# A decode step on one core: the first K chunk is loaded in two parts, with the first query weights between them

## The chip, the cores and the metric

The kernel runs on one NeuronCore of a Trainium2 chip. The metric is the device time of one execution in microseconds (us). The engines are TensorE (PE; its weight loads are listed as PEld), VectorE (DVE), ScalarE (ACT), GpSimd (POOL) and SyncE (SP). SyncE issues nearly all loads; the core's sixteen DMA engines carry them out.

## The reference

One token passes a transformer block: attention over a cache of 65,536 positions (32 query heads in 8 groups of 4, one K and one V head for each group), then a gated feed-forward layer. Everything is float32.

```python
# x (1, 1, 512); k_cache, v_cache (1, 8, 65536, 128); wq (512, 4096); wo (4096, 512)
q = (layernorm(x) @ wq)                      # 32 heads of 128
scores = einsum("bhqd,bhkd->bhqk", q, repeat(k, 4)) * 128 ** -0.5
o = einsum("bhqk,bhkd->bhqd", softmax(scores), repeat(v, 4))
h = x + o.reshape(1, 1, 4096) @ wo
n = layernorm(h)
out = h + ((n @ w_gate) * (n @ w_up)) @ w_down   # 512 -> 1792 -> 512
```

K and V hold 268 MB each, so every execution reads some 565 MB.

## The kernel before

The cache is cut by head and by chunk. A chunk is 16,384 positions of one K or V head, laid out by the host as 128 rows of 64 KB, one row for each SBUF partition, 8 MiB in all. A head has four K chunks and then four V chunks. Two buffers, `kv[0]` and `kv[1]`, take the chunks in turn. In K chunks the partition is the head dimension, so every score matmul needs all 128 rows of its columns.

The program is written by hand, one stream of instructions for each engine, with semaphores between them. Python unrolls the streams of SyncE, VectorE and ScalarE over the 8 heads; TensorE runs `head()` in a hardware loop.

SyncE's stream (lines 111 to 147) is a list of loads in one queue. It starts with `wq_sb`, the query weights of head 0 (128 rows of 8 KB, 1 MiB, line 111, semaphore `s_wq`). Then come the chunks, line 131, each behind a wait until TensorE is done with the chunk two places before, since that one had the same buffer. The first two chunks need no such wait. Two chunks before the end of a head, the weights for the output of this head and the query of the next follow (line 121; line 123 for the last head). The last V chunk of all and the feed-forward weights come in pieces, so that the last matmuls can begin early.

TensorE first helps with the layer norm of x (lines 320 to 326), waits for constants from VectorE and for the query weights (`take(s_wq, 16)`, which waits for the count and takes it off again), and enters the loop. In `head()` it computes the query of a head with 16 small matmuls (line 333), waits for VectorE to copy it into `q_pad`, waits for chunk 0 on `s_kv[0]`, and runs 32 matmuls of 512 columns on it (line 343); the same for chunks 1 to 3. After the softmax come the four V chunks (line 371), then the output projection into `attn`.

A DMA adds 16 to its semaphore when all of it has landed. The semaphores `s_kv[0]` and `s_kv[1]` belong to the buffers; `s_wq` is used once in the program.

## Time and profile before

| | before |
|---|---|
| median of 3 runs | 1309.71 us (1309.70 to 1309.72) |
| profiled execution | 1309.92 us |
| its span, first to last instruction | 1308.5 us |
| mean granted TensorE clock | 0.738 |
| DMA in all | 564.80 MB, 432 GB/s over the span |
| busy share of TensorE | 54% |

The busy times, durations and waits in the text come from one profiled execution. "Granted clock" is the share of full speed that TensorE was given. In a row of the timeline the columns are start in us, duration in us, engine, line, operation and operands, how many, and in brackets how long the engine stood idle before and what ended that. In a row of DMA issues they are operands, issuing queue, operation, count, size of one where given, and the median time from issue to landing where the profile has one. A queue's row gives packets, megabytes and the share of the sixteen DMA engines' time.

### The profile page before, as it was taken

The numbers are of one execution on the slowest core, as the hardware profiler recorded it, in microseconds if no ns is written. First come the engines' busy times: TensorE is split into PE (matmuls) and PEld (weight loads), VectorE is DVE, ScalarE is ACT, GpSimd is POOL, SyncE is SP. The second block draws the span as 40 slices with busy tenths as digits, with TensorE's granted clock in tenths as the row PEclk, the third lists the DMA queues.
The fourth block names the chain that finished last, engine by engine and source line by source line (L and its number), as shares of the span: only waits on it lengthen the run. The fifth ranks groups of instructions, "written<-read, shape, count | busy, mean of one in ns | idle before, by whom it ended". The sixth has DMA issues, their size and how long they took to land. (4 is left out here: it accounts for less than half of the span.)

```text
span 1308.5 us, 10559 instructions
## 1 busy us (share of the span) xinstructions
PE 712.9 (54%) x4938; PEld 249.0 (19%) x4938; DVE 73.5 (6%) x181; ACT 47.2 (4%) x102; POOL 2.5 (0%) x13
## 2 busy tenths in 40 slices
PE   5366384553755446563564636636365465655556
PEld 3012031210312112120131202212021121311113
DVE  0000000100001000010000100001000010000101
ACT  0000000100001000010000100001000010000100
POOL 0000000000000000000000000000000000000000
PEclk9777666776767867767767867678677677687778
DMA  9999999999999999999999999999999999999998
GB/s 417 427 435 445 421 445 425 441 425 441 425 441 425 441 429 441 441 429 437 429 439 427 441 425 441 427 441 437 435 435 431 439 417 450 425 441 425 441 420 374
DMA packets 12260, 564.80 MB, mean 432 GB/s; under 512 B 1365, under 2 KB 1369, under 8 KB 2010
## 3 DMA queue, kind: packets, MB, share of 16 engines
q1 hardware_dynamic: 12248, 564.67, 99.7%
q8 instruction: 6, 0.10, 0.0%
q14 instruction: 4, 0.03, 0.0%
q10 hardware_dynamic: 2, 0.00, 0.0%
HBM read 564.66 MB, written 0.00 MB: 432 GB/s over the span
## 5 line engine op out<-in xcount | busy, mean ns | idle before, releaser
L343 PE MATMUL psc<-kv,q_pad 128*32 128x512 f32 x2048 | 294.6, 740 | 256.2 <-PEq L315 256.2
L371 PE MATMUL pva<-kv,pt 128*16 128x512 f32 x2048 | 280.1, 707 | 276.9 <-PEq L315 276.8
L343 PEld LDWEIGHTS psc<-kv,q_pad 128*32 128x32 f32 x2048 | 81.3, 133 | 463.0 <-issue 463.0
L371 PEld LDWEIGHTS pva<-kv,pt 128*16 128x16 f32 x2048 | 67.1, 110 | 492.7 <-issue 492.7
L210 ACT COPY sc<-psc 128x512 f32<-128x512 f32 x32 | 18.7, 585 | 1144.3 <-PE psc L343 1144.3
L216 DVE TENSOR_REDUCE mx<-sc 128x1 f32<-128x512 f32 x32 | 21.9, 686 | 538.3 <-ACT sc L210 538.3
L333 PEld LDWEIGHTS sm<-xn,wqo_sb 128*128 128x128 f32 x256 | 49.1, 299 | 10.4 <-issue 10.4
L333 PE MATMUL sm<-xn,wqo_sb 128*128 128x1 f32 x256 | 49.8, 329 | 2.2 <-issue 2.2
L250 DVE COPY orow<-pva 128x512 f32<-128x512 f32 x8 | 5.5, 692 | 566.8 <-PE pva L371 566.8
L358 PE MATMUL ptp<-ident,sc 128*128 128x128 f32 x128 | 29.3, 396 | 10.2 <-PEq L315 9.7
L358 PEld LDWEIGHTS ptp<-ident,sc 128*128 128x128 f32 x128 | 21.4, 202 | 15.5 <-issue 14.7
L235 ACT ACTIVATE sc<-sc,nbias 128x512 f32<-128x512 f32 x32 | 22.7, 711 | 20.2 <-DVE nbias L230 20.2
L240 DVE COPY pt<-ptp 128x512 f32<-128x512 f32 x32 | 22.1, 691 | 21.6 <-PE ptp L358 21.6
L363 PE MATMUL pva<-zeros 128*32 128x512 f32 x64 | 12.9, 890 | 0.0
L384 PE MATMUL attn<-wqo_sb,o_pad 128*32 128x512 f32 x64 | 10.8, 749 | 3.4 <-PEq L315 3.4
L378 PE MATMUL sm<-sel_b,orow 128*128 128x4 f32 x64 | 8.2, 252 | 7.2 <-PEq L315 7.2
L378 PEld LDWEIGHTS sm<-sel_b,orow 128*128 128x128 f32 x64 | 7.7, 191 | 14.4 <-issue 14.4
L349 PE MATMUL sm<-ident,m 128*1 128x128 f32 x8 | 2.2, 269 | 13.6 <-PEq L315 13.6
L406 PE MATMUL psc<-kv,hn_pad 128*32 128x448 f32 x64 | 8.2, 651 | 1.9 <-DMA kv<-in_wu 1.0
L361 PE MATMUL sm<-l,ones 128*128 128x4 f32 x16 | 3.9, 312 | 9.6 <-PEq L315 9.6
L351 PE MATMUL sm<-ones,mexp 1*128 1x1 f32 x16 | 3.4, 279 | 5.7 <-PEq L315 5.7
L235 ACT ACTIVATION_READ_ACCUMULATOR sc<-sc,nbias 128x1 f32 x32 | 6.0, 187 | 0.0
(88 smaller groups left out, 68.6 us busy)
## 6 DMA issues: line engine op xcount, KB each, us to landing
wqo_sb<-in_wqo SPq DMA_DIRECT2D x7, 2048.0 KB, 15.2
kv<-in_v SPq DMA_DIRECT2D x1, 4096.0 KB, 21.7
kv<-in_wg SPq DMA_DIRECT2D x1, 3584.0 KB, 18.8
kv<-in_v SPq DMA_DIRECT2D x1, 2048.0 KB, 26.2
kv<-in_v SPq DMA_DIRECT2D x2, 1024.0 KB, 29.1
kv<-in_wu SPq DMA_DIRECT2D x1, 1792.0 KB, 23.0
kv<-in_wu SPq DMA_DIRECT2D x2, 896.0 KB, 25.5
kv<-in_wd SPq DMA_DIRECT2D x1, 1536.0 KB, 19.7
```

What stands on the lines that cost most here:

```text
L210: copies.append(act.tick(act_e.copy(sc[s], psc[s % 2])))
L216: i = dve_e.tensor_reduce(out=mx[:, s:s + 1], in_=sc[s], axis=AX.X, op=ALU.max)
L235: act_e.activation(sc[s], sc[s], AF.Exp, bias=nbias[:, 0:1], scale=SCALE, accum_out=sums[:, s:s + 1]).then_inc(atok, 1)
L240: dve_e.tensor_copy(pt[s].rearrange("p g b h -> p b g h"), ptp[s % 2].rearrange("p (b g h) -> p b g h", b=4, h=REP)).then_inc(tok, 1)
L333: i = mm(sm[0][:, r:r + 1], wq_sb[:, k, r * P:(r + 1) * P], xn[:, k:k + 1], start=(k == 0), stop=(k == KT - 1))
L343: i = mm(psc[s % 2][32 * j:32 * j + 32, :], q_pad[:, 28 - 4 * rs:60 - 4 * rs], kv[s % 2][:, (4 * rs + j) * 512:(4 * rs + j + 1) * 512], st ...
L358: i = pe_e.transpose(ptp[s % 2][:, b * P:(b + 1) * P], sc[s][:, b * P:(b + 1) * P], ident)
L363: mm(pva[32 * j:32 * j + 32, :], zeros[:, 0:32], zeros, start=True, stop=False)
L371: i = mm(pva[32 * j:32 * j + 16, :], pt[n][:, 8 * j + rs, :, :].rearrange("p b h -> p (b h)"), vt[:, w * 512:(w + 1) * 512], start=False, ...
L378: i = mm(sm[0][:, 0:REP], orow[:, b * P:(b + 1) * P], sel_b[:, 4 * b:4 * b + 4], start=(b == 0), stop=(b == 3))
L384: i = mm(attn[32 * r:32 * r + 32, :], o_pad[:, r, :], wo_sb[:, r, :], start=True, stop=True)
L406: i = mm(acc[32 * j:32 * j + 32, :FJ], hn_pad[:, k, :], w[:, o:o + FJ], start=(k == 0), stop=(k == KT - 1))
```

## The change

Chunk 0 of head 0 is no longer one load. Its rows 0 to 15 are the first load of the program, the query weights the second, and its rows 16 to 127 the third. The 16 rows count on the semaphore of the weights, and TensorE waits for both (32 instead of 16) ahead of its loop. `s_kv[0]` gets its 16 from the load of the 112 rows. The bytes, the destination and everything after chunk 0 are unchanged.

```diff
-    sp.dma_start(wq_sb, wq0).then_inc(s_wq, 16)
     done = []
     for h in range(HKV):
         for i in range(2 * NT):
...
-            if h == LAST and i == 2 * NT - 1:
+            if not done:
+                sp.dma_start(kv[0][0:16], kT[0, 0][0:16]).then_inc(s_wq, 16)
+                sp.dma_start(wq_sb, wq0).then_inc(s_wq, 16)
+                sp.dma_start(kv[0][16:P], kT[0, 0][16:P]).then_inc(s_kv[0], 16)
+            elif h == LAST and i == 2 * NT - 1:
...
     pe_e.wait_ge(dve.sem, c_const)
-    take(s_wq, 16)
+    take(s_wq, 32)
```

## The prediction

> **What bounds the kernel now.** I read the page of the profile first: the engine totals, the forty slices and the DMA queues.

> ```profile
> span 1308.5 us, 10559 instructions
> PE 712.9 (54%) x4938; PEld 249.0 (19%) x4938; DVE 73.5 (6%) x181; ACT 47.2 (4%) x102; POOL 2.5 (0%) x13
> DMA  9999999999999999999999999999999999999998
> DMA packets 12260, 564.80 MB, mean 432 GB/s; under 512 B 1365, under 2 KB 1369, under 8 KB 2010
> q1 hardware_dynamic: 12248, 564.67, 99.7%
> ```

> TensorE is busy for 54% of the span and no other compute engine for over 6%. The DMA row is the one without a hole: the sixteen DMA engines are busy nine tenths or more in 39 slices of 40, and SyncE's queue alone fills 99.7% of their time. 564.67 MB at 432 GB/s is 1307 us, which is the span. So the kernel is as long as its loads, and time lost on the DMA engines has no idle time later in which to be made up.

> The next view is the DMA issues, with the summary of line 131, which issues the whole chunks of K and V.

> ```profile
> kv<-in_kT SPq DMA_DIRECT2D x32, 29.2
> kv<-in_v SPq DMA_DIRECT2D x31, 29.9
> wqo_sb<-in_wq SPq DMA_DIRECT2D x1, 1024.0 KB, 4.8
> x_row<-in_xr ACTq DMA_DIRECT2D x1, 2.0 KB
> out_y<-y SPq DMA_DIRECT2D x1, 2.0 KB
> DMA to landing us min/median/max: 23.7/29.4/44.1
> ```

> A chunk is 128 rows of 64 KB, 8.39 MB, and takes 8.39 / 432 = 19.4 us at the mean rate. The median chunk lands 29.4 us after its issue, so it stands about 10 us in the queue behind the chunk before. That is why a late start is not absorbed: when everything slides by some us, each landing, each release by TensorE and each new issue slide with it, and the engines still have work queued.

> The chain of waits, in order of time, shows the same at the end.

> ```profile
> 1283.06 22.84 DMA kv<-in_wd
> 1305.90 0.04 issue
> 1305.94 0.47 PE pva L437 x8
> 1306.41 0.02 issue
> 1306.44 0.29 DVE y L297
> ```

> The last weights land at 1305.90 and under 1 us of arithmetic follows. A shift of the DMA stream is a shift of the end, one for one.

> **The change part by part.** The start is where the edit is. These are rows of the timeline of its first 60 us, then two stretches of the table of windows (their last columns are the granted clock, the DMA share and GB/s).

> ```profile
> 0.73 0.40 SPq L111 DMA_DIRECT2D wqo_sb<-in_wq  x1
> 1.20 53.85 SPq L131 DMA_DIRECT2D kv<-in_kT  x4
> 8.40 0.15 DVE L200 COPY sel_pad<-sel 128x1 f32<-128x1 f32 x1
> 8.93 6.98 PE L333 MATMUL sm<-xn,wqo_sb 128*128 128x1 f32 x32 [2.24 <-issue]
> 15.94 0.16 DVE L213 COPY q_pad<-sm 128x4 f32<-128x4 f32 x1 [7.08 <-PE sm L333]
> 25.01 9.00 PE L343 MATMUL psc<-kv,q_pad 128*32 128x512 f32 x64 [9.11 <-PEq L315]
> 0.00:5.00 5.00, 2.28 (x10) 2.23 (x10) 0.63 (x5) 1.28 (x1) 2.48 (x13) 1.00 0.72 263
> 200.00:300.00 100.00, 50.50 (x349) 15.21 (x349) 6.11 (x14) 4.69 (x11) 0.00 (x0) 0.72 1.00 435
> ```

> One more issue on SyncE. Three loads are issued where there were two. The first took 0.40 us; one more of that size puts the issues of the remaining 112 rows and of chunk 1 about 0.4 us later. The engines then hold the 1 MiB loads in front, 2 x 2.43 us of work (1.05 MB at 432 GB/s each). Cost nothing; without that cover 0.4 us. Nothing is moved on the queues of ScalarE or GpSimd, and no later issue changes.

> The wait for the query weights. TensorE now waits for the 16 rows and the weights together. Before, the weights landed at 0.73 + 4.8 = 5.5 us, and their matmuls began at 8.93, behind the constants that VectorE finished at 8.55: 3.4 us to spare. If the 16 rows take 2.43 us, the weights land at 8.0 and nothing moves. If they take t us, the weights land near 5.5 + t, the query is ready 7.0 + 0.2 us after that, and behind TensorE's wait stands only the work on chunk 0. That chunk comes by the same queue behind the weights and its other 112 rows alone need 7/8 of 19.4 = 17.0 us; 17.0 exceeds 7.2, so the query is always ready first. Cost nothing, whatever t is.

> The 16-row load itself. Same bytes, but they now go to partitions 0 to 15 alone. Every large load of this trace covers all 128 partitions; the narrow ones, one row of x and the output, are 2 KB and show no rate. So bound it from both sides. If only the sixteen DMA engines matter, they take a 64 KB row each at full rate: 2.43 us, no cost. If 432 GB/s is what 128 partitions can take in, 16 of them take an eighth of it and the load lasts as long as a whole chunk, 19.4 us: 17.0 lost. While it lasts nothing else can go, since the weights and the 112 rows stand behind it in the same queue on the same engines. Between factors 1 and 8 no row lies nearer to one end; I take a factor of 4, about the middle: 9.7 us, 7.3 lost. [...]

> The 112-row load. Shared among sixteen engines it is 7 rows an engine instead of 8, so 17.0 us if all go at full rate. [...] Lower bound nothing; with two engines on one way throughout, a factor of 2, 17.0 us lost on the engine that fares worst, and a load has landed only when its last engine is done. [...] An engine that falls behind here has the same bytes left as before and stays behind to the end.

> At the start-up there might be a gain. In the first 5 us 263 GB/s flowed, 1.32 MB, which at 432 GB/s is 3.04 us: 1.96 us went without flow, 0.73 of them ahead of the first issue. A first load with fewer rows could start flowing earlier, by at most 1.2 us and at least nothing; I take nothing.

> Sum: 0 + 0 + 7.3 + 8.5 + 0 = 15.8 us. The profiled execution took 1309.92 us (span 1308.5 and 1.42 around it), so 1325.7; the median of the runs, 1309.71, is 0.21 lower, so **1325.5 us**.

> **The rivals.** The forecast: both loads are slowed, by 12 to 24.3 us together (7.3 plus 5 to 17.0; or 17.0 and little after it, which gives 1326.7 and is told apart by the landing of the 16 rows). For it: the change leaves 112 partitions idle on a resource that is full for 99.7% of the time.

> Only the first load is slow (7 to 12 us, about 1317.0 by 7.3 alone). This is so if the engines are dealt the 112 rows as evenly as the 128. It decides at the place where the 112-row load ends: all engines done within 17 us of their start.

> Not slower. The DMA engines, not the partitions, are the limit: sixteen rows keep sixteen engines at full rate, both small loads pass in 4.9 us, and the only difference left is the earlier first flow, 0 to 1.2 us: 1308.5 to 1309.7. It decides if the 16 rows land within about 5 us of their issue, as the 1 MiB of weights did in 4.8. For it: an engine's share of 64 KB is the same in both loads. Against it: nothing in the trace, which has no narrow load of size. [...]

> Much slower. If the 112 rows are dealt row by row, so that at each moment sixteen adjacent rows are written, each seventh goes at the factor 4 of the first load: 7 x 9.7 = 67.9 in place of 17.0, 50.9 lost, with 7.3 before it 58 us: 1367.7. Or both upper bounds hold, 17.0 + 17.0: 1343.7. Against the first: in the wide loads sixteen engines together keep 435 GB/s (the second window), so their rows are not dealt in a way that collides.

> **How the numbers follow.** I give the forecast 0.58, only the first load slow 0.22, not slower 0.11, much slower 0.09. The range from 1316 to 1334 holds the first two: it starts a little below 7.3 lost and ends at 7.3 + 17.0 = 24.3 lost. It leaves out 0.20. A measurement of this kernel tells a difference from none at about 0.2%, 2.6 us. Both slow cases and the much slower one are beyond it: slower 0.89. The whole gain to be had at the start is 1.2 us, so the not-slower case is almost all within it: same 0.10, faster 0.01.

> **What would show it.** Right: the 16-row load lands 10 to 13 us after its issue (about 9.7 and the start-up of some 2.4 that the weights' load had: 4.8 less 2.43); the query's matmuls move from 8.93 to some 16 us, without consequence; chunk 0's scores begin near 41 us instead of 25.01; chunks follow at the old pace; the last weights land some 16 us later; q1's share falls because single engines wait. Wrong: the 16 rows land within 5 us; or chunk 0's scores begin at 32 us (first load alone) or beyond 50 us; or the delay at chunk 0 is there but is smaller at the end, which would mean that the stream has slack that I have not seen.

## The result and the profile after

The changed kernel takes 1331.08 us (median of 5 runs, 1330.26 to 1331.56) against 1309.70 for the kernel before on the same chip: 21.4 us more, a ratio of 1.0161 with a 95% interval of 1.0151 to 1.0172. The profiled execution took 1331.56 us with a span of 1330.2. So it is slower, as forecast, by more than the 15.8 us of the sum and inside the range.

From the page of the kernel after, the span, the DMA slices, the GB/s slices, and SyncE's queue; below them the GB/s slices of the kernel before:

```profile
span 1330.2 us, 10560 instructions
DMA  9999999999999999999999999999999999999998
GB/s 221 353 434 434 441 434 426 437 437 436 424 440 436 433 428 437 436 437 436 428 434 439 434 428 439 436 434 428 438 436 437 434 430 434 439 432 430 439 417 361
q1 hardware_dynamic: 12264, 564.67, 99.6%
```

```profile
GB/s 417 427 435 445 421 445 425 441 425 441 425 441 425 441 429 441 441 429 437 429 439 427 441 425 441 427 441 437 435 435 431 439 417 450 425 441 425 441 420 374
```

A slice is 33 us here. The first ran at 221 GB/s and the second at 353, where the kernel before has 417 and 427; from the third on, the rate is the old one. The row of busy shares shows nothing of this: the share is the time that the packets took, however slow they were, so 99.6% stands where 99.7% stood, and from 15 to 45 us the share is 0.95 at 238 GB/s where the kernel before has 0.97 at 418. The GB/s row has to be read beside it.

The start in the timeline of the kernel after (lines are three to four further down than before; L124, L125 and L126 are the three loads), and the summaries of the three loads, in that order:

```profile
0.74 0.41 SPq L124 DMA_DIRECT2D kv<-in_kT  x1
1.21 0.40 SPq L125 DMA_DIRECT2D wqo_sb<-in_wq  x1
1.65 0.43 SPq L126 DMA_DIRECT2D kv<-in_kT  x1
15.79 6.97 PE L336 MATMUL sm<-xn,wqo_sb 128*128 128x1 f32 x32 [9.09 <-PEq L318]
22.80 0.16 DVE L216 COPY q_pad<-sm 128x4 f32<-128x4 f32 x1 [13.93 <-PE sm L336]
47.47 8.98 PE L346 MATMUL psc<-kv,q_pad 128*32 128x512 f32 x64 [24.71 <-PEq L318]
```

```profile
DMA to landing us min/median/max: 11.9/11.9/11.9
DMA to landing us min/median/max: 14.2/14.2/14.2
DMA to landing us min/median/max: 45.7/45.7/45.7
```

The 16 rows land at 0.74 + 11.9 = 12.6 us, the weights at 15.4, the 112 rows at 47.4. The query is ready at 23.0, and TensorE, whose last query matmul ended at 22.76, stands idle for 24.71 us until chunk 0 is there. The scores of chunk 0 begin at 47.47 where they began at 25.01: 22.5 us later. The end of the chain moves nearly as far: the last weights land at 1327.60 instead of 1305.90, 21.7 us later.

```profile
1304.96 22.64 DMA kv<-in_wd
1327.60 0.04 issue
1327.64 0.47 PE pva L440 x8
```

Two stretches of the windows table tell how the 112 rows went (last column: GB/s), first of the kernel after, then of the kernel before:

```profile
15.00:30.00 15.00, 6.97 (x32) 6.90 (x32) 0.16 (x1) 0.00 (x0) 0.00 (x0) 1.00 0.79 210
30.00:45.00 15.00, 0.00 (x0) 0.00 (x0) 0.00 (x0) 0.00 (x0) 0.00 (x0) 1.00 1.10 267
```

```profile
15.00:30.00 15.00, 5.89 (x37) 2.25 (x40) 0.16 (x1) 0.00 (x0) 0.00 (x0) 1.00 0.97 419
30.00:45.00 15.00, 4.01 (x40) 1.05 (x32) 0.69 (x1) 0.58 (x1) 0.00 (x0) 0.81 0.96 416
```

Together the sixteen engines ran at half rate and a little over it. The trace's packets, one for each row, show that all of them did: in the load of 112 rows a row took 2.8 to 4.9 us (median 4.5), where a row of a whole chunk takes 2.42 in the kernel before. It is not one engine that fell behind. In the first load the sixteen rows, moved side by side, took 8.0 to 9.2 us each.

### The profile page after: what moved, and what is told of

Same layout as the page of the kernel before. It is cut to its first block, busy times and chain, and to the rows that moved or that the text cites. A ratio compares the mean times of both kernels' runs of the same rounds, so it can differ in the third digit from the quotient of the medians.

```text
span 1330.2 us, 10560 instructions
## 1 busy us (share of the span) xinstructions
PE 718.0 (54%) x4938; PEld 250.7 (19%) x4938; DVE 73.5 (6%) x181; ACT 47.2 (4%) x102; POOL 2.5 (0%) x13
## 2 busy tenths in 40 slices
DMA  9999999999999999999999999999999999999998
DMA packets 12276, 564.80 MB, mean 425 GB/s; under 512 B 1381, under 2 KB 1385, under 8 KB 2026
## 3 DMA queue, kind: packets, MB, share of 16 engines
q1 hardware_dynamic: 12264, 564.67, 99.6%
## 5 line engine op out<-in xcount | busy, mean ns | idle before, releaser
L213 ACT COPY sc<-psc 128x512 f32<-128x512 f32 x32 | 18.7, 585 | 1166.6 <-PE psc L346 1166.6
L361 PE MATMUL ptp<-ident,sc 128*128 128x128 f32 x128 | 29.1, 394 | 10.2 <-PEq L318 9.7
L243 DVE COPY pt<-ptp 128x512 f32<-128x512 f32 x32 | 22.1, 691 | 21.4 <-PE ptp L361 21.4
## 6 DMA issues: line engine op xcount, KB each, us to landing
kv<-in_v SPq DMA_DIRECT2D x1, 4096.0 KB, 21.4
kv<-in_v SPq DMA_DIRECT2D x2, 1024.0 KB, 28.9
```

Of the source, the lines that this page charges most:

```text
L213: copies.append(act.tick(act_e.copy(sc[s], psc[s % 2])))
L243: dve_e.tensor_copy(pt[s].rearrange("p g b h -> p b g h"), ptp[s % 2].rearrange("p (b g h) -> p b g h", b=4, h=REP)).then_inc(tok, 1)
L361: i = pe_e.transpose(ptp[s % 2][:, b * P:(b + 1) * P], sc[s][:, b * P:(b + 1) * P], ident)
```

## The experiments

The theory was that the partitions a load writes set its rate. Its rivals were the cut as such (a third load, a small one first, a later wait of TensorE), the order, and the source rows in memory. "Way in" or "way" stands in the prediction and the expectations for whatever several partitions may share when they are written. It is a supposition: the runs show what sets of partitions cost, not such a way.

**The same cut, by columns.**

```diff
-                sp.dma_start(kv[0][0:16], kT[0, 0][0:16]).then_inc(s_wq, 16)
+                sp.dma_start(kv[0][:, 0:2048], kT[0, 0][:, 0:2048]).then_inc(s_wq, 16)
                 sp.dma_start(wq_sb, wq0).then_inc(s_wq, 16)
-                sp.dma_start(kv[0][16:P], kT[0, 0][16:P]).then_inc(s_kv[0], 16)
+                sp.dma_start(kv[0][:, 2048:], kT[0, 0][:, 2048:]).then_inc(s_kv[0], 16)
```

> The same three loads in the same order, with the same sizes, semaphores and waits as in the changed kernel, but chunk 0 is cut by columns: columns 0 to 2047 of all 128 rows (1 MiB), the query weights, then the other 14,336 columns (7 MiB). Partition theory (few or unevenly dealt partitions take data slowly): nothing is lost, 1309.7 within 0.5 us either way, the first load lands about 4.8 us after its issue. Rival, the split theory (a third load, the small one first, or the later wait of TensorE costs it, whatever the rows): as the changed kernel, 1331.

Measured: 1310.00 us against 1309.91 for the kernel before, ratio 1.0000 (0.9991 to 1.0009). The loads of the same sizes land after 4.9, 6.9 and 23.3 us:

```profile
DMA to landing us min/median/max: 4.9/4.9/4.9
DMA to landing us min/median/max: 6.9/6.9/6.9
DMA to landing us min/median/max: 23.3/23.3/23.3
```

So three loads, a small one first, and the sizes of 1 and 7 MiB cost nothing. What is left is that the loads take part of the rows.

**The order.**

```diff
-                sp.dma_start(kv[0][0:16], kT[0, 0][0:16]).then_inc(s_wq, 16)
                 sp.dma_start(wq_sb, wq0).then_inc(s_wq, 16)
+                sp.dma_start(kv[0][0:16], kT[0, 0][0:16]).then_inc(s_wq, 16)
```

> The changed kernel with its first two loads exchanged: query weights, then rows 0 to 15, then rows 16 to 127. Partition theory: the same narrow loads, the same 21 us lost, 1331. Rival, the wait theory (the query comes late because the weights stand behind the rows): partly or wholly undone, towards 1309.7.

Measured: 1331.60 us, ratio 1.0164 (1.0149 to 1.0180). The order of the first two loads is worth nothing. The run does not test the wait, though: TensorE still waits for both loads, and its query matmuls begin at 15.73 us as before. That the wait is harmless is seen in the row of chunk 0 above and in the last experiment below.

**Each load by itself.** The kernel before gets one load more, ahead of all, into the second buffer, which chunk 1 overwrites later. Nobody reads the data. The second run has `kv[1][16:P], kT[0, 0][16:P]`.

```diff
+    sp.dma_start(kv[1][0:16], kT[0, 0][0:16]).then_inc(s_x, 16)
     sp.dma_start(wq_sb, wq0).then_inc(s_wq, 16)
...
+            if len(done) == 1:
+                sp.wait_ge(s_x, 16)
```

> The kernel before with one load more ahead of all others: rows 0 to 15 of chunk 0 into partitions 0 to 15 of the second buffer, data that nobody reads; chunk 1 is issued to that buffer after it has landed. Its time above 1309.7 is the cost of a 16-row load by itself. Partition theory: the 9.9 us by which the weights landed later in the changed kernel (15.4 against 5.5), so 1319.6; it lands 11.9 us after its issue. Rival, all is lost in the 112-row load: 1 MiB at full rate, 2.4 us, 1312.1.

> As the run with the extra 16 rows, but the extra load is rows 16 to 127 into partitions 16 to 127 of the second buffer, 7 MiB that nobody reads. Partition theory: the 31.9 us between the landing of the weights and of the 112 rows in the changed kernel, so 1341.6. Rival, the 112 rows were slow only because the 16-row load ahead had put the DMA engines out of step: 7 MiB at full rate, 17.0 us, 1326.7.

Measured: 1319.15 us with the 16 rows and 1340.15 with the 112 rows against 1309.91, that is 9.2 and 30.2 us (ratios 1.0070, 1.0055 to 1.0086, and 1.0230, 1.0214 to 1.0246). At 432 GB/s their bytes would take 2.4 and 17.0 us. So 6.8 us are lost in the 16 rows and 13.2 in the 112 rows, which are slow without the narrow load ahead of them. In the summaries the two extra loads land after 12.1 and 33.7 us:

```profile
DMA to landing us min/median/max: 12.1/12.1/12.1
DMA to landing us min/median/max: 33.7/33.7/33.7
```

**Source or destination.** The 16 extra rows once with the destination spread (`kv[1][0:P:8], kT[0, 0][0:16]`) and once with the source spread (`kv[1][0:16], kT[0, 0][0:P:8]`).

> The run with 16 extra rows ahead of all, but into partitions 0, 8, 16 to 120 of the second buffer; the source is the same 16 adjacent rows (the data is read by nobody). Partition theory: dearer than 2.4 us only as far as these partitions still share ways in. [...] With ways shared by neighbours alone: 2.4 us, 1312.2. Rival, the source theory (16 adjacent rows of 64 KB are slow to read from memory): as the 16 adjacent partitions, 9.2 us, 1319.1.

> The run with 16 extra rows into partitions 0 to 15, but the source is every eighth row of the chunk instead of 16 adjacent ones (the data is read by nobody). Partition theory: unchanged, 9.2 us above the kernel before, 1319.1. Rival, the source theory: as a row of a wide load, 2.4 us, 1312.2.

Measured: with the destination spread 1314.80 against 1309.85, 4.9 us (median of eight runs, ratio 1.0048, 1.0029 to 1.0066); with the source spread 1318.87, 9.0 us (1.0069, 1.0052 to 1.0086), landing 11.9 us after its issue as in the changed kernel. For these 16 rows the destination decides, 4.9 us against 9.2; spreading the source leaves 9.0. That the spread rows still cost 4.9 us and not the 2.4 of their bytes is not explained by neighbours alone.

The first two of the eight executions with the destination spread took 1325.5 and 1324.1 us, some 10 us more than the other six, so the kernel was run six times more. The same 4.9 us were expected; the median was 1314.88 against 1309.78, 5.1 us (1.0038, 1.0023 to 1.0052), but one execution took 1323.3. No other kernel here had such executions, and the kept profiles of this one are of two of them. In both the extra load lands after 7.8 and 7.9 us, and most of the excess arises behind it: up to some 85 us into the span, a row of a chunk takes 2.79 and 2.71 us in place of 2.42. From 50 to 100 us, first such an execution, then the run with 16 adjacent rows (last column: GB/s):

```profile
50.00:100.00 50.00, 18.45 (x128) 5.07 (x128) 1.37 (x2) 1.17 (x2) 0.00 (x0) 0.67 0.97 379
50.00:100.00 50.00, 24.29 (x160) 6.77 (x164) 1.37 (x2) 1.17 (x2) 0.00 (x0) 0.68 1.01 438
```

Whether the narrow load brings this about is not known. The medians, and so the 4.9 and 5.1 us, rest on the executions without it.

**Sixty-four rows, three ways.** The extra load has 64 rows, rows 0 to 63 of the chunk each time. They go to partitions 0 to 63 (`kv[1][0:64]`), then 0, 2 to 126 (`kv[1][0:P:2]`), then 32 to 95 (`kv[1][32:96]`).

> An extra load of 64 rows (4 MiB, read by nobody) into partitions 0 to 63, ahead of all others. At full rate 9.7 us, 1319.6. [...]

> The same 64 rows of source, but into partitions 0, 2, 4 to 126 of the second buffer, so that together they reach every way in. If it matters which partitions a load reaches in all: full rate, 9.7 us, 1319.6. [...]

> The extra 64 rows (4 MiB, read by nobody) into the adjacent partitions 32 to 95. [...]

Measured: 20.3 us for 0 to 63 (1330.15 against 1309.85, ratio 1.0155, 1.0138 to 1.0172); 10.1 us for 0, 2 to 126 (1319.97; 1.0078, 1.0061 to 1.0094); 10.2 us for 32 to 95 (1319.95 against 1309.78; 1.0078, 1.0061 to 1.0095). The windows from 2 us to near the end of the load, in the same order:

```profile
2.00:21.00 19.00, 2.98 (x12) 2.78 (x12) 2.76 (x15) 0.81 (x2) 1.23 (x6) 1.00 1.07 221
```

```profile
2.00:12.00 10.00, 2.97 (x12) 2.77 (x12) 2.77 (x15) 0.82 (x2) 1.23 (x6) 1.00 1.03 419
```

```profile
2.00:12.00 10.00, 2.97 (x12) 2.77 (x12) 2.77 (x15) 0.82 (x2) 1.24 (x6) 1.00 1.03 419
```

The first went at 221 GB/s, about half rate, the other two at 419; at the full rate of 432 GB/s their bytes take 9.7 us. So a load of fewer than 128 rows need not be slow. Why the first set is and the other two are not, no run shows.

**Ninety-six rows** (`kv[1][32:P], kT[0, 0][32:P]`, partitions 32 to 127).

> An extra load of 96 rows (6 MiB, read by nobody) into partitions 32 to 127, 6 rows an engine. At full rate 14.5 us, 1324.3. [...]

Measured: 1339.38 against 1309.87, 29.5 us (ratio 1.0227, 1.0209 to 1.0244), twice the 14.6 us of its bytes. The packets say the same: each of the 96 rows took 3.8 to 5.2 us, about twice the 2.42 of a whole chunk's rows. In two of their three places the loads of 64 rows show none of it (10.1 and 10.2 us for 9.7).

**A cut by rows, every fourth row to one load.**

```diff
-                sp.dma_start(kv[0][0:16], kT[0, 0][0:16]).then_inc(s_wq, 16)
+                sp.dma_start(kv[0][0:P:4], kT[0, 0][0:P:4]).then_inc(s_wq, 16)
                 sp.dma_start(wq_sb, wq0).then_inc(s_wq, 16)
-                sp.dma_start(kv[0][16:P], kT[0, 0][16:P]).then_inc(s_kv[0], 16)
+                sp.dma_start(kv[0][1:P:4], kT[0, 0][1:P:4]).then_inc(s_wq, 16)
+                sp.dma_start(kv[0][2:P:4], kT[0, 0][2:P:4]).then_inc(s_x, 16)
+                sp.dma_start(kv[0][3:P:4], kT[0, 0][3:P:4]).then_inc(s_kv[0], 16)
...
-    take(s_wq, 32)
+    take(s_wq, 48)
+    take(s_x, 16)
```

> The changed kernel with another choice of rows: the first load is every fourth row of chunk 0 (partitions 0, 4 to 124, 2 MiB), the query weights follow, then the other three quarters in the same way. TensorE waits for the weights and three of the four loads before its loop, so the query is ready near 26 us and chunk 0 starts 1 to 2 us later than in the kernel before, which the queue behind it covers. [...] Rival, any load of fewer than 128 rows loses: at a factor of 2 on the chunk, 19 us, 1329.

Measured: 1310.40 against 1309.78, ratio 1.0005 (0.9995 to 1.0014), 0.6 us, which the interval does not tell from nothing. Chunk 0 is cut by rows into four loads and next to nothing is lost. The timeline of this run also settles the wait:

```profile
20.97 6.98 PE L340 MATMUL sm<-xn,wqo_sb 128*128 128x1 f32 x32 [14.41 <-PEq L321]
28.45 8.73 PE L350 MATMUL psc<-kv,q_pad 128*32 128x512 f32 x64 [0.50 <-PEq L321]
```

The query matmuls begin 5 us later than in the changed kernel and chunk 0's scores wait for them, since its last rows landed at 25.4. They begin 3.4 us behind the kernel before, more than the 1 to 2 expected, and the end moves by 0.6.

The extra loads side by side; the full-rate time is their bytes at 432 GB/s:

| partitions of the extra load | added us | at full rate | factor |
|---|---|---|---|
| 0 to 15 | 9.2 | 2.4 | 3.8 |
| 0, 8 to 120 | 4.9 and 5.1 | 2.4 | 2.1 |
| 0 to 63 | 20.3 | 9.7 | 2.1 |
| 0, 2 to 126 | 10.1 | 9.7 | 1.0 |
| 32 to 95 | 10.2 | 9.7 | 1.0 |
| 32 to 127 | 29.5 | 14.6 | 2.0 |
| 16 to 127 | 30.2 | 17.0 | 1.8 |

No version beats the kernel before; the best cut only equals it.

## Why the prediction was right, and where it was not

What bounds the kernel: right. The scores of chunk 0 moved by 22.5 us and the last landing by 21.7; a loss on the DMA engines at the start comes out at the end. The two extra loads show the same in a kernel that is otherwise untouched.

The third issue on SyncE: right at nothing. The cut by columns has the same issues and adds 0.1 us.

The wait for the weights: right at nothing. The matmuls moved to 15.79, forecast as some 16, and 24.7 us of waiting for chunk 0 lay behind them.

The 16-row load: right in kind and size. I took a factor of 4 and 7.3 us lost; by itself it shows 3.8 and 6.8, and its landing, forecast at 10 to 13 us, came at 11.9. The kind was argued, but the 4 was only the middle between 1 and 8, which no row of the trace favoured, so the close size is partly luck.

The 112-row load: right in kind, too small. This is the term of the sum that was mis-sized: 8.5 us, half of the bound of 17.0. No run shows the 8.5, nor the two engines on one way of its bound; it was my estimate, and the runs showed 14.9 and 13.2 us in its place. In the changed kernel the 112 rows needed 47.35 - 15.41 = 31.9 us behind the weights, 14.9 over the 17.0 of their bytes, a factor of 1.88 where I took 1.5. With 6.8 for the 16 rows this makes 21.7, against 21.4 measured. By itself the load loses 13.2, so 1.7 us come only behind the other two; the cause of that was not tried.

The bound was taken for the engine that fares worst, but the windows and packets show all sixteen slowed together, at 210 and then 267 GB/s in place of 419 and 416. Chunk 0's scores, forecast near 41 us, began at 47.47.

That q1's share would fall was wrong as a sign: it hardly moved, 99.6% after 99.7%, because a slow packet's whole time counts, 4.5 us (median) for a row of the 112 in place of 2.42.

The gain at the start-up: none, as taken. The first packet of SyncE's queue starts 1.78 us into the span, in the kernel before 1.76.

The rivals: "not slower" fell with the landing of the 16 rows at 11.9 us, "only the first load" with the 31.9 us of the 112 rows, "much slower" with a factor of 1.9 for the 112 rows in place of 4 and with 6.8 us lost in the 16 rows in place of 17.0.

Open is which partitions slow a load, and how its rows are dealt to the DMA engines: a packet of the trace has a queue, a size and times, but no engine and no partition. The runs give the cost of seven sets of partitions, from full rate (10.1 and 10.2 us for 9.7) to a factor of 3.8 (9.2 us for 2.4), and none of them shows a rule behind the seven.

## What to carry to other kernels

Cut a load by columns and keep all 128 partitions in each part; the same cut by rows cost 21 us here and the cut by columns 0.1. If rows must be cut, take every fourth partition rather than a block: four such loads cost 0.6 us, not told from nothing. In a kernel whose DMA engines never rest, read the GB/s row and not the busy share (0.95 at 238 GB/s here, 0.97 at 418 before), and count a slow first load in full at the end (the scores of chunk 0 came 22.5 us later, the last weights 21.7).
